# The opening of a long-convolution kernel in one written order, with half-array convolution and turns

## The chip, the cores and the metric

The kernel runs on one core of one Trainium2 chip. The metric is the device time of one execution in microseconds (us); the median of the timed runs counts, and a profiled execution shows where its time goes. The engines are TensorE (PE in the profile, its weight loads PEld), VectorE (DVE), ScalarE (ACT), GpSimd (POOL) and SyncE (SP, which only issues DMAs here).

## The reference

Two layers, each a long convolution block and a dense block, forward and backward. The transforms of the convolution are along time; `kv` and its spectrum depend on no layer's input, so both layers share them.

```python
def _A_ref(q, k, v, shift_k, ssm_k, ssm_D):
    B, S, D = q.shape                      # 1, 2048, 448
    ks = shift_k.shape[-1]                 # 4
    k_pad = jnp.pad(k, ((0, 0), (ks - 1, 0), (0, 0)))
    k_shift = jnp.zeros_like(k)
    for t in range(ks):
        k_shift = k_shift + k_pad[:, t:t + S, :] * shift_k[:, ks - 1 - t][None, None, :]
    kv = k_shift * v
    kv_f = rfft(pad(kv, S), axis=time)     # length 2 S
    kf_f = rfft(pad(ssm_k, S))
    y = irfft(kv_f * kf_f)[:, :S] + kv * ssm_D
    return q * y

def _B_ref(x, w1, w2):
    return silu(x @ w1) @ w2               # D = 448 to F = 1792 and back

x = A_q
x = x + _A_ref(_layernorm(x), A_k, A_v, A_shift_k, A_ssm_k, A_ssm_D)
x = x + _B_ref(_layernorm(x), B_w1, B_w2)
x = x + _A_ref(_layernorm(x), A_k, A_v, A_shift_k, A_ssm_k, A_ssm_D)
x = x + _B_ref(_layernorm(x), B_w1, B_w2)
# outputs: x, and its gradients by grad_out in q, k, v, shift_k, ssm_k, ssm_D, w1, w2
```

## The kernel before

The kernel has three stages. The **opening** (`_ssm_prefix`, L342 on) computes the product of two spectra and turns it back as far as `A1kv`. The **main part** (`Main`) runs the layers forward and backward, with TensorE's order written out by hand. The **suffix** does the gradients of the convolution. The change is in the opening, and in one late load and product that read what the opening stored (L1353 and L1383).

The 4096-point transform is split 128 x 16. A stage of 128 points is a matmul by `M1sb`, a stage of 16 points with real and imaginary parts is a matmul by a 128x128 matrix (`Gsb`, `Gpre`), and between the two the data is turned on TensorE (a "turn" is a set of transposes into PSUM and a copy out of it). All of this passes through PSUM: one tile of four (tag `A`) per step, filled by TensorE and emptied by ACT or DVE. The steps of the opening, with the letters that the written orders use:

- A, a: `ssm_k` (`ksd`, `K_sb`) turned into `Kt` (L398 to L409); D adds `ssm_D` to its first row; B, b: first stage into `A1K` (L411 to L419), which is one half of the array `KAB`.
- G: 16 diagonal matrices 112x112 of the shift's weights (L431). T, t: `k_n` turned into `kT` (L448), 129 positions a row so that a shift by one row of blocks is an offset of one column. C, c: the shifted sum as matmuls of `kT` by the diagonals into `ps_cv` and a copy to `ks` (L467, L470); O: its store `KS_d` (L472); m: its product with `v_n` (L473). S, s: first stage of that into `A1kv` (L483).
- K, k: five groups of `A1K` turned into `Z`, on the halves of the array (L232), and two by DMA (KD, L442). P, p: second stage in place (14 pieces of 1024 columns, L251); Q: for two pieces the store `spec_K` and four DMAs that swap halves into `KAB[:, 0]` (L289).
- Z, z: seven groups of `A1kv` turned into `ZkvA`, `ZkvB` (L542); F, f: second stage in place; U: the stores `spec_KV`, behind two of which the loads of `w1sb` and `w2sb` are issued (L561, L567).
- M: the spectra's products, `pab` (DVE, L572); V, v: the inverse second stage (L260, L261) and the copy to `A1kv`.
- N: the layer norm of the first rows in steps; W: `w2T` by DMA transposes (L452, L453), `Minvsb` (L218) and `gb0` (L516).

In a token of a written order a capital is the work of TensorE or of the issuing engine, a small letter the copy, and its last letter `a` or `d` the engine (ACT, DVE); the numbers name the piece.

Before, the program from the first turn up to about P8 is written as loops, for which the scheduler sets the order of each engine; a load balancer (`_Bal.pick`, L98) gives each copy to ACT or DVE by its estimate of their load. In the loops the channels (d) are split in halves of 224 and in four blocks of 112. Only from there on does `PRODUCTS` fix the order of PE, ACT, DVE and POOL. SP has no written order. `w2T`, `Minvsb` and `gb0` are issued on SP behind the two DMA turns.

Behind the opening, `ys` (L599, `ps_y`) needs all of `A1kv`; then `ps_g` needs `w2T` and `ps_h` needs `w1sb`.

Of the kernel before, what the change touches and what calls it, by code (L numbers as in the profile page):

```python
# [10 lines left out]
FP32 = mybir.dt.float32  # L11
# [6 lines left out]
P = 128  # L18
# [103 lines left out]
PRODUCTS = """  # L122
P9 P10 P11 P12 p9a p10d p11a P13 p12d P8 p8a Z0 Q5 p13d Z1 z0d Z2 z1a Q6 F0 z2d F1 f0a F2 f1d F3 f2a F4 Q4 M0 F5 f3a Z4
f4a Z6 z4d f5a z6d F8 f8a F9 M1 F12 F13 f9a Z5 M2 f12a V0 z5d f13a Z3 v0a F11 z3yd z3xd F7 f11a M3 F6 f7a F10 V1 M4 f6a
V2 f10a M6 V3 v1a M5 V4 v2a M11 V5 v3a V6 M10 v4a V11 M12 v5a V10 M13 v6a V12 v11a M7 V13 v10a M8 V7 v12a M9 V8 v13a v8d
V9 v7a v9a
# [16 lines left out]
def kernel(  # L143
# [33 lines left out]
    k.KS_d = dram.tile([2, P, J, D // 2], BF16, name="KS_d")  # L177
# [87 lines left out]
def _fft_inv_stage2_half(k, pa, pb, B1, ci, psum, cnd):  # L265
    nc = k.nc
    pv = psum.tile([P, 2, 8, 64], FP32, name="ps_v", **k.pt["v"])
    for i in range(8):
        for src, g, first in ((pa, G_IAC, True), (pb, G_IBC, False)):
            for r in range(2):  # L270
                ri = slice(64 * r, 64 * r + 64)
                nc.tensor.matmul(pv[:, r ^ (ci & 1), i, :], lhsT=src[ri, i * P:(i + 1) * P], rhs=k.Gsb[ri, g, ri], start=first, stop=not first)  # L272
    out = (B1[:, :, 32 * ci:32 * ci + 32].rearrange("p q (i h s) -> p h i q s", h=2, s=2) if cnd
           else B1[:, 8 * ci:8 * ci + 8, :].rearrange("p i (q h s) -> p h i q s", h=2, s=2))
    _copy(nc, k.bal.pick(1024), out, pv[:].rearrange("p h i (q s) -> p h i q s", s=2))
# [43 lines left out]
def _ln_steps(k, pool, c, src, si, n_g):  # L319
# [4 lines left out]
    for tl in range(4):  # L324
        k.tc.keep_in_program_order(nc.vector.bn_stats(out=st[:, tl, :], in_=src(tl)))
# [5 lines left out]
        yield  # L331
    for tl in range(4):
        k.tc.keep_in_program_order(nc.vector.tensor_scalar(out=n_g[:, tl, :], in0=src(tl), scalar1=mv[:, tl, 0:1], scalar2=r[:, tl:tl + 1], op0=ALU.subtract, op1=ALU.mult))
        yield
# [6 lines left out]
def _ssm_prefix(k):  # L341
# [4 lines left out]
    with ExitStack() as es:  # L346
# [6 lines left out]
        k.M1sb = k.wk.tile([P, 16, 2, P], BF16, name="M1sb", tag="WX")  # L353
# [15 lines left out]
        skc = spec.tile([DC, ND, 4], FP32, name="skc")  # L369
        skb = spec.tile([DC, ND, 4], BF16, name="skb")  # L370
# [1069 lines left out]
```

## Time and profile before

| | us |
|---|---|
| median of three timed runs | 697.8 (697.25 to 698.92) |
| the profiled execution | 692.97 |
| its span, first to last instruction | 690.9 |
| last copy into `A1kv` ends | 84.7 |
| first `ps_y`, first `ps_g`, first `ps_h` | 84.77, 90.56, 96.47 |

The granted TensorE clock was 0.999 of full speed over the span. A row of the timeline gives start, length, engine, line, operation, what it writes and reads, its shape and how many such instructions follow one another; a length covers them all. Idle time ahead of an instruction stands in square brackets with what ended it. In a table of windows each engine has its busy time and its instructions in brackets; matmuls overlap, so PE's busy time is more than its work. Rows of SPq, ACTq and POOLq are DMAs being issued; the DMA view adds the time from issue to landing.

### The profile page before, as it was taken

The page shows a single profiled execution, that of the slowest core. Times are in us where ns is not written, and L with a number is a line of the kernel's source. Part 1 is how long each engine was busy: PE and PEld are TensorE (multiplying, and loading weights), DVE is VectorE, ACT ScalarE, POOL GpSimd, SP SyncE. Part 2 cuts the span into 40 slices and gives each one's busy share as a digit, 9 for nine tenths or more (in the row PEclk, how much of TensorE's full clock was granted, in tenths as well). Part 3 has the DMA queues.
Part 4 walks back from the last instruction along what each step waited for, and adds up shares of the span by engine and source line. Part 5 has one row for each costly group of instructions (what it writes and reads, how often), then busy time and mean ns, then how long its engine had stood idle before and what let it go on. Part 6 is the DMA issues. An engine that isn't in the chain of part 4 may idle for free.

```text
span 690.9 us, 14461 instructions
## 1 busy us (share of the span) xinstructions
PE 669.0 (97%) x5844; PEld 362.1 (52%) x5879; DVE 481.6 (70%) x1131; ACT 429.9 (62%) x522; POOL 104.8 (15%) x177
## 2 busy tenths in 40 slices
PE   8999999899999999999999999999999999999997
PEld 6876745454434444444444444544555555555666
DVE  5779943667889858899478874843936555538992
ACT  5988976878947868669577585223543543554431
POOL 1057310110011100111001000010111211102311
PEclk9999999999999999999999999999999999999999
DMA  8999978179698777597766789949599988957991
GB/s 320 244 316 321 337 203 220 56 191 259 167 265 233 221 182 176 137 253 219 199 157 183 211 231 354 271 142 210 191 249 342 328 285 315 341 190 223 320 310 42
DMA packets 203956, 162.60 MB, mean 235 GB/s; under 512 B 153505, under 2 KB 184244, under 8 KB 203122
## 3 DMA queue, kind: packets, MB, share of 16 engines
q1 hardware_dynamic: 190806, 113.35, 60.2%
q0 software_dynamic: 11088, 39.84, 16.7%
q10 hardware_dynamic: 1996, 8.49, 3.7%
q8 instruction: 46, 0.75, 0.5%
q14 instruction: 20, 0.16, 0.1%
HBM read 66.05 MB, written 54.60 MB: 175 GB/s over the span
## 4 chain that ended last, share of the span: by engine, by line
PE 64%; DVE 19%; issue 6%; ACT 5%; DMA 3%; POOL 3%; POOLq 0%; ACTq 0%
PE ps_d L1082 25%; PE ps_n L872 8%; PE ps_h L674 6%; PE ps_g L674 6%; PE ps_o L834 5%; DVE ln_st L308 2%; DVE lb_v L1030 2%; PE ps_v L272 2%; POOL rstd L313 2%; DMA spec_K<-KAB 1%; DVE n L316 1%; DVE lb_v L1033 1%; DVE lb_v L1034 1%; DVE X L838 1%; PE ps_h L678 1%
## 5 line engine op out<-in xcount | busy, mean ns | idle before, releaser
L1082 PEld LDWEIGHTS <-dstat 128*128 128x128 bf16 x928 | 87.1, 98 | 75.7 <-issue 4.0
L872 PE MATMUL ps_n<-w1T,ghT 128*128 128x448 bf16 x448 | 96.6, 353 | 2.0 <-DVE ghT L857 1.7
L834 PE MATMUL ps_o<-w2sb,aT 128*128 128x448 bf16 x448 | 89.2, 353 | 0.6 <-DVE X L838 0.6
L674 PE MATMUL ps_h<-nT,w1sb 128*128 128x512 bf16 (+1 forms) x410 | 83.5, 336 | 2.2 <-ACT Dall L116 1.0
L116 ACT CAST ghT<-ps_g 128x1024 bf16<-128x1024 f32 (+1 forms) x54 | 48.4, 900 | 58.3 <-PE ps_g L678 47.7
L674 PE MATMUL ps_g<-nT,w2T 128*128 128x512 bf16 x317 | 77.9, 379 | 2.2 <-DVE Dall L117 0.5
L872 PEld LDWEIGHTS <-ghT 128*128 128x128 bf16 x448 | 41.4, 98 | 50.7 <-DVE ghT L857 6.7
L834 PEld LDWEIGHTS <-aT 128*128 128x128 bf16 x448 | 43.2, 98 | 41.1 <-issue 2.7
L674 PEld LDWEIGHTS <-w1sb 128*128 128x128 bf16 x420 | 39.2, 98 | 36.7 <-issue 7.2
L817 ACT ACTIVATE aT<-ps_h 128x1024 bf16<-128x1024 f32 (+1 forms) x48 | 44.2, 921 | 19.1 <-PE ps_h L674 10.2
L1030 DVE SCALAR_TENSOR_TENSOR lb_v<-lb_u,n 128x448 bf16<-128x448 bf16 x60 | 37.2, 620 | 24.5 <-ACT lb_u L876 24.1
L116 ACT CAST Dall<-ps_h 128x1024 bf16<-128x1024 f32 (+2 forms) x60 | 54.3, 904 | 0.0
L313 POOL TENSOR_TENSOR rstd<-ln_ve,mhalf 128x2 f32<-128x2 f32 (+1 forms) x24 | 19.9, 831 | 225.7 <-DVE ln_ve L312 225.7
L674 PEld LDWEIGHTS <-w2T 128*128 128x128 bf16 x336 | 31.3, 98 | 42.1 <-issue 7.2
L827 ACT ACTIVATE Dall<-Dall 128x1024 bf16<-128x1024 bf16 (+1 forms) x48 | 53.2, 1186 | 0.1
L1082 PE MATMUL ps_d<-X,dstat 128*128 128x448 bf16 x224 | 47.6, 353 | 0.0
L1082 PE MATMUL ps_d<-go,dstat 128*128 128x448 bf16 x224 | 47.2, 353 | 0.0
L1082 PE MATMUL ps_d<-n3m,dstat 128*128 128x448 bf16 (+1 forms) x240 | 47.0, 340 | 0.0
L1082 PE MATMUL ps_d<-n1m,dstat 128*128 128x448 bf16 (+1 forms) x240 | 46.5, 340 | 0.0
L876 ACT ACTIVATE lb_u<-ps_n,rstd 128x448 bf16<-128x448 f32 x32 | 20.5, 640 | 28.9 <-PE ps_n L872 24.3
L116 ACT CAST A1g<-ps_v 128x1024 bf16<-128x1024 f32 x14 | 15.0, 1069 | 36.5 <-PE ps_v L272 36.5
L838 DVE TENSOR_TENSOR X<-X,ps_o 128x448 bf16<-128x448 bf16 x32 | 19.5, 611 | 21.3 <-PE ps_o L834 21.1
(210 smaller groups left out, 1112.4 us busy)
## 6 DMA issues: line engine op xcount, KB each, us to landing
dstat<-a_d SPq DMA_DIRECT2D x28, 512.0 KB, 5.2
dstat<-g_d SPq DMA_DIRECT2D x28, 512.0 KB, 5.8
a_d<-turned SPq DMA_DIRECT2D x16, 512.0 KB, 3.0
g_d<-turned SPq DMA_DIRECT2D x16, 512.0 KB, 3.0
a_d<-turned SPq DMA_DIRECT2D x16, 384.0 KB, 2.7
g_d<-turned SPq DMA_DIRECT2D x16, 384.0 KB, 3.0
spec_K<-KAB POOLq DMA_DIRECT2D x7, 512.0 KB, 5.7
KAB<-KAB POOLq DMA_DIRECT2D x28, 128.0 KB, 5.1
```

The costliest lines, as they stand in the source:

```text
L116: return nc.scalar.copy(out, in_)
L272: nc.tensor.matmul(pv[:, r ^ (ci & 1), i, :], lhsT=src[ri, i * P:(i + 1) * P], rhs=k.Gsb[ri, g, ri], start=first, stop=not first)
L313: nc.gpsimd.tensor_tensor(out=r[:, lo:hi], in0=ve[:, lo:hi], in1=k.mhalf[:, lo:hi], op=ALU.pow)
L674: self.nc.tensor.matmul(ps, lhsT=w[:, b, ft * P:(ft + 1) * P], rhs=x[:, b], start=(start and b == 0), stop=(stop and b == bs[2]))
L817: self.last_silu = nc.scalar.activation(aT[hh][:, o:o + hi - lo, :], ps(lo, hi), ACT.Silu)
L827: self.nc.scalar.activation(dT[hh][:, o:o + n, :], dT[hh][:, o:o + n, :], ACT.Derivative_silu)
L834: nc.tensor.matmul(po[:, :D], lhsT=aT[ft // 7][:, ft % 7, tl * P:(tl + 1) * P], rhs=self.w2sb[:, ft, :], start=(ft == 0), stop=(ft == NF - 1))
L838: self.last_o = nc.vector.tensor_tensor(out=X[:, t, :], in0=X[:, t, :], in1=po[:, :D], op=ALU.add)
L872: nc.tensor.matmul(pn[:, :D], lhsT=gh[ft // 7][:, ft % 7, tl * P:(tl + 1) * P], rhs=self.w1T[:, ft, :], start=(ft == 0), stop=(ft == NF - 1))
L876: nc.scalar.activation(u0[:], pn[:, :D], ACT.Identity, scale=k.rstd[2 * L + 1][:, t:t + 1], accum_out=cp[:, tl, 0:1])
L1030: nc.vector.scalar_tensor_tensor(out=v[:], in0=u0, scalar=-1.0 / D, in1=n_t, op0=ALU.mult, op1=ALU.mult, accum_out=cp[:, 1:2])
L1082: self.nc.tensor.matmul(ps[:, cols], lhsT=st[:, t, :], rhs=mov[:, t, cols], start=(first and t == 0), stop=(last and t == NT - 1))
```

## The change

One order, `OPENING`, replaces the loops and `PRODUCTS`; it covers everything from A0 to the last copy into `A1kv` and fixes PE, ACT, DVE, POOL and SP. Who copies is written into the tokens, and the balancer is out of use there. A token with `h` works on the halves of the array (64 rows of weights at a time, the two halves in turn). With it:

- The channels are split at 256 (CH), and `k_n` is turned in four blocks of 128 (the last overlaps the third); the convolution multiplies 64 rows by 64x64 diagonals: 64 matmuls a piece for h = 0, 48 for h = 1, in place of 32 of 112 rows.
- The diagonals come from two broadcast products (G) on DVE, not from 16 instructions; the `skc` cast on POOL goes, and the shifts come by two loads.
- T3, T0, T2, the K turns, six of seven Z turns, and V4, V11 and V12 are on halves. `kT` is copied out in one piece a turn.
- T stands ahead of part of B; Z0 and Z2 stand ahead of the last piece of S. P, K, C and S are interleaved piece by piece.
- On SP: the two DMA turns, `Minvsb`, `gb0`, the store U0, then w2's two transposes, ahead of which they were before.
- `KS_d` is one array, not two halves; the loads and products that read it follow.

The core of the diff:

```diff
-PRODUCTS = """
...
+OPENING = """
+A0 a0xa G1 A1 a1xd D0 a0ya B01 a1ya B00 b00a B02 A2 b01d G0 a2d B03 b02a b03a A3 a3d B04 b04a B05 b05d B15 B16 B07
+b07d D1 T3h t3d b15a b16a T0h t0a T1 B06 b06a t1d T2h C00 c00a O00 C11 c11a O11 t2d B10 B13 b10a B11 b11a m00 b13d m11
+C03 c03a B17 b17d m03 S110 s110a B12 b12a K0h C12 S001 c12a O12 s001a B14 b14a k0d N0 K2h S030 s030a O03 K1h m12 k2d
+S111 S000 k1d N1 C10 s111a s000a c10a C01 c01a K3h N2 N3 k3d P1 p1a P3 p3a P2 p2d Q1 P4 p4a S031 m01 S120 s031a K4h
+C02 s120a m10 c02a O02 S010 k4d O01 s010d S011 s011a P5 p5d P7 p7a m02 S121 s121a C13 S101 s101a S020 s020a S021 c13d
+O10 m13 P8 p8a s021d S130 s130d P9 KD5 Z0h z0d p9a S100 s100a P0 p0a KD6 W4 W0 Z2h S131 P6 Q2 s131a N4 z2d Q4 Z3h z3xd
+P11 O13 Q0 z3yd P10 N5 p6a Q3 Z4h F0 z4d p11a p10a Z1h Q5 f0a z1d N6 P13 F9 p13a f9a Z5h P12 p12a Q6 F8 F1 z5d f1a U0
+W1 W2 F4 f8d f4d F3 f3a F11 f11a F2 F7 F5 f7a M8 M3 f2a U2 U7 f5a Z6 z6d F6 f6a M0 V3 U6 M4 V8 v3a v8a F10 M9 f10a M6
+F13 F12 f13a f12a V0 V9 V4h M7 M10 V7 U4 v0a V6 M2 v9a V10 v4a V2 M1 U11 M13 M5 M11 U9 v7a v6a v10a v2a V1 v1a V13 V5
+M12 N7 v5d v13a V11h v11a V12h v12a U13
 """
...
-    k.KS_d = dram.tile([2, P, J, D // 2], BF16, name="KS_d")
+    k.KS_d = dram.tile([P, J, D], BF16, name="KS_d")
...
-        k.M1sb = k.wk.tile([P, 16, 2, P], BF16, name="M1sb", tag="WX")
+        m1t = k.wk.tile([P, 16 * 2 * P + ND * 4 * 64], BF16, name="M1sb", tag="WX")
+        k.M1sb = m1t[:, 0:16 * 2 * P].rearrange("p (n c k) -> p n c k", c=2, k=P)
...
-        kT = k.wk.tile([DC, 4, ND, 4, 129], BF16, name="kT", tag="W1")
-        w2o = k.wk.tile([P, 2 * S + ND * 4 * DC], BF16, name="ksd", tag="W2")
+        kT = k.wk.tile([P, 4, ND, 4, 129], BF16, name="kT", tag="W1")
+        w2o = k.wk.tile([P, 2 * S], BF16, name="ksd", tag="W2")
         ksb = [w2o[:, i * S:(i + 1) * S] for i in range(2)]
         ksb += [_hd(k, [P, S], "K_sb")[:] for i in range(2)]
-        diag = w2o[:DC, 2 * S:].rearrange("p (c j d) -> p c j d", c=ND, j=4)
+        diag = m1t[:, 16 * 2 * P:].rearrange("p (c j d) -> p c j d", c=ND, j=4)
...
+        nc.scalar.dma_start(out=skb[:, 0:3, :], in_=k.A_shift_k[0:384, :].rearrange("(c p) j -> p c j", p=P))
+        nc.scalar.dma_start(out=skb[64:128, 3, :], in_=k.A_shift_k[384:448, :])
...
+        CH = ((0, 256), (256, 448))
+        H2 = SPEC // 2
...
+        def A_(part):
+            lo, hi = KPARTS[part]
             n = hi - lo
-            kview = ksb[lo // P][:n].rearrange("p (n1 n2) -> p n2 n1", n2=16)
-            pt = psum.tile([P, 2, 1024], BF16, name="ps_kt", **a_)
-            pv = pt[:, :, 0:8 * n].rearrange("p g (i d) -> p g i d", d=n)
+            kview = ksb[part][:n].rearrange("p (n1 n2) -> p n2 n1", n2=16)
+            pv = bank(("a", part), [P, 2, 1024], "ps_kt", BF16)[:, :, 0:8 * n].rearrange("p g (i d) -> p g i d", d=n)
             for i in range(16):
                 nc.tensor.transpose(pv[:, i // 8, i % 8, :], kview[:, i, :], k.ident[:n, :n])
...
+
+        def a(part, s, e):
+            lo, hi = KPARTS[part]
+            n = hi - lo
+            pv = live["a", part][:, :, 0:8 * n].rearrange("p g (i d) -> p g i d", d=n)
+            gs = {"": slice(0, 2), "x": slice(0, 1), "y": slice(1, 2)}[s]
+            _copy(nc, e, Kt.rearrange("p (g i) d -> p g i d", g=2)[:, gs, :, lo:hi], pv[:, gs])
...
+        def B_(h, i):
+            lo, hi = CH[h]
+            ps = bank(("b", h, i), [P, 2, 2, 256], "ps_s1")
+            for w in range(2):
+                for c in range(2):
+                    nc.tensor.matmul(ps[:, w, c, :hi - lo], lhsT=k.M1sb[:, 2 * i + w, c, :], rhs=Kt[:, 2 * i + w, lo:hi], start=True, stop=True)
...
+        def G_(r):
+            n, rs = 3 + r, slice(64 * r, 64 * r + 64)
+            nc.vector.tensor_tensor(out=diag[rs, 0:n].rearrange("p c j d -> p (c j) d"),
+                                    in0=k.ident[rs, rs].rearrange("p (o d) -> p o d", o=1).broadcast_to((64, 4 * n, 64)),
+                                    in1=skb[rs, 0:n].rearrange("p c (j o) -> p (c j) o", o=1).broadcast_to((64, 4 * n, 64)), op=ALU.mult)
...
+        def turned(key, name, srcs, half):
+            if half:
+                pt = bank(key, [P, 2, 16, 64], name, BF16)
+                for i in range(16):
+                    _turn64(k, pt, i, srcs(i))
+                live[key] = pt[:].rearrange("p r i x -> p i r x")
+            else:
+                pt = bank(key, [P, 16, P], name, BF16)
+                for i in range(16):
+                    nc.tensor.transpose(pt[:, i, :], srcs(i), k.ident[:])
+                live[key] = pt[:].rearrange("p i (r x) -> p i r x", r=2)
...
+        def T_(jq, half):
+            turned(("t", jq), "ps_kT", lambda i: kn[:, 4 * jq + i % 4, GBLK[i // 4][0]:GBLK[i // 4][1]], half)
+
+        def t(jq, s, e):
+            _copy(nc, e, kT[:, jq].rearrange("p c j q -> p (c j) q")[:, :, 1:129].rearrange("p i (r x) -> p r i x", r=2), live["t", jq].rearrange("p i r x -> p r i x"))
...
+        def K_(g, half):
+            turned(("k", g), "ps_tr", lambda i: A1Kf[:, 16 * g + i, :], half)
...
+        def C_(h, jq):
+            pc = bank(("c", h, jq), [P, 4, 4, 64], "ps_cv")
+            at = {(0, 0): 0, (0, 1): 2, (1, 0): 1, (1, 1): 3} if h == 0 else {(2, 0): 1, (2, 1): 2, (3, 1): 3}
             for u in range(4):
                 j = 4 * jq + u
...
+                for e in (2 * h, 2 * h + 1):
+                    for q in range(4):
+                        js = (j - q) % J
+                        src = kT[:, js // 4, e, js % 4, 1:129] if j >= q else kT[:, js // 4, e, js % 4, 0:128]
+                        for r in range(2):
+                            if (e, r) in at:
+                                rs = slice(64 * r, 64 * r + 64)
+                                nc.tensor.matmul(pc[:, at[e, r], u, :], lhsT=src[rs], rhs=diag[rs, e, q, :], start=(q == 0), stop=(q == 3))
...
+        def c_(h, jq, s, e):
+            lo, hi = CH[h]
+            kk = work.tile([P, 2, 4, 256], BF16, name="ks_kv", tag="pab", bufs=4)
+            ks, kvt = kk[:, 0, :, :hi - lo], kk[:, 1, :, :hi - lo]
+            live["m", h, jq] = ks, kvt
+            pc = live["c", h, jq]
+            if h == 0:
+                _copy(nc, e, ks.rearrange("p u (e r d) -> p r e u d", e=2, r=2), pc[:].rearrange("p (r e) u d -> p r e u d", r=2))
+            else:
+                _copy(nc, e, ks.rearrange("p u (x d) -> p x u d", x=3), pc[:, 1:4])
...
+        def O_(h, jq):
+            nc.gpsimd.dma_start(out=k.KS_d[:, 4 * jq:4 * jq + 4, CH[h][0]:CH[h][1]], in_=live["m", h, jq][0])
+
+        def m(h, jq):
+            ks, kvt = live["m", h, jq]
+            nc.vector.tensor_tensor(out=kvt, in0=ks, in1=vn[:, 4 * jq:4 * jq + 4, CH[h][0]:CH[h][1]], op=ALU.mult)
...
+        def U_(lo):
+            hi = min(x for x in (2, 4, 6, 7, 9, 11, 13, 14) if x > lo)
+            (nc.gpsimd if lo else nc.sync).dma_start(out=k.SPEC_d["KV"][:, lo * 1024:hi * 1024], in_=zkv(lo * 1024, hi * 1024))
...
+        def V_(ci, half):
             pab = live["V", ci]
...
+            if half:
+                live["v", ci] = _fft_inv_half(k, pab[:, 1], pab[:, 0], ci, psum)[:].rearrange("p h i (q s) -> p h i q s", s=2)
+            else:
+                live["v", ci] = _fft_inv_stage2_full(k, pab[:, 1], pab[:, 0], ci, psum)[:]
+            live["vh", ci] = half
...
+        def W(i):
+            if i == 0:
+                k.gb0 = _hd(k, [P, 4, D], "gb0")
+                nc.sync.dma_start(out=k.gb0[:], in_=_pm(k.grad_out[0])[:, 0:4, :])
+            elif i == 1:
+                k.w2T = k.wk.tile([P, ND, F], BF16, name="w2T", tag="WY")
+                nc.sync.dma_start_transpose(out=k.w2T[:, 0:3, :], in_=k.B_w2[:, 0:384])
+            elif i == 2:
+                nc.sync.dma_start_transpose(out=k.w2T[:, 3:4, :], in_=k.B_w2[:, 320:448])
+            else:
+                _load_minv(k, nc.sync)
...
+        flat = {"P", "p", "F", "f", "U", "M", "V", "v"}
+        with tc.manual_schedule(engines={e.engine for e in (nc.tensor, nc.scalar, nc.vector, nc.gpsimd, nc.sync)}):
+            for tok in OPENING.split():
+                kind = tok[:next(i for i, x in enumerate(tok) if x.isdigit())]
+                rest = tok[len(kind):]
+                num = "".join(x for x in rest if x.isdigit())
+                args = [int(num)] if kind in flat else [int(x) for x in num]
+                tail = rest[len(num):]
+                if kind in "abtkcszpfv":
+                    args += [tail[:-1], eng[tail[-1]]]
+                elif kind in "TKZV":
+                    args.append(tail == "h")
+                do[kind](*args)
...
-                ksf = sp.tile([P, 2, J, D // 2], BF16, name="ksf")
+                ksf = sp.tile([P, J, D], BF16, name="ksf")
                 with tc.issue_after(k.last_x.ins):
-                    nc.scalar.dma_start(out=ksf[:], in_=k.KS_d[:].rearrange("h p j d -> p h j d"))
+                    nc.scalar.dma_start(out=ksf[:], in_=k.KS_d[:])
```

More of the change, by code (lines that the diff above doesn't have):

```diff
@@ L537, in Q, with Z_ @@
             _swap_halves_dma(k, KAB[:, 0, :], Ka, lo, hi)
-        def Z_(g):
-            pt = live["z", g] = psum.tile([P, 16, P], BF16, name="ps_tr", **a_)
-            for i in range(16):
-                nc.tensor.transpose(pt[:, i, :], B1[:, 16 * g + i, :], k.ident[:])
-        def z(g, part, eng):
-            lo, hi = (8 * part, 8 * part + 8) if g == 3 else (0, 16)
-            _copy(nc, eng, block(g, lo, hi), live["z", g][:, lo:hi, :])
+        def Z_(g, half):
+            turned(("z", g), "ps_tr", lambda i: B1[:, 16 * g + i, :], half)
@@ L590, in _ssm_prefix @@
+        k.xq.append(live["xq"])
         B1v = B1.rearrange("p a (c n s) -> p a c n s", c=2, n=16)
```

233 lines of the change are left out of this document (77 added, 156 removed).

## The prediction

> **What bounds the kernel now.** I read the page's head first, then the opening in windows of 5 us, the engines in order of time there, and the wait view of the first 86 us.
>
> ```profile
> span 690.9 us, 14461 instructions
> ...
> PE 669.0 (97%) x5844; PEld 362.1 (52%) x5879; DVE 481.6 (70%) x1131; ACT 429.9 (62%) x522; POOL 104.8 (15%) x177
> ```
>
> TensorE (PE) carries the whole kernel, so a stage ahead of the main part is worth what it ends earlier. The opening hands over when the last copy into `A1kv` is done, at 84.7 us (ACT, 83.71 + 1.01); the first `ps_y` matmul starts at 84.77. The lists of both programs have the same order on every engine from `ps_y` on, so I count each microsecond of the opening as one of the total. The windows (length, busy time and instructions of PE, PEld, DVE, ACT, POOL, then the granted clock, the DMA share and GB/s):
>
> ```profile
> 30.00:35.00 5.00, 4.83 (x105) 4.64 (x105) 3.64 (x7) 5.00 (x6) 1.10 (x2) 1.00 1.28 191
> 45.00:50.00 5.00, 4.83 (x63) 3.77 (x62) 3.06 (x4) 3.88 (x6) 2.93 (x7) 1.00 1.03 343
> 70.00:75.00 5.00, 4.99 (x75) 4.31 (x75) 5.00 (x6) 5.00 (x7) 3.49 (x7) 1.00 1.00 348
> 75.00:80.00 5.00, 5.00 (x92) 4.93 (x90) 5.00 (x5) 5.00 (x6) 1.65 (x2) 1.00 0.99 317
> 90.00:95.00 5.00, 4.53 (x27) 2.14 (x27) 4.29 (x13) 3.60 (x5) 1.47 (x2) 1.00 0.14 49
> ```
>
> In the last stretch both copy engines, ACT and VectorE (DVE), are full; in the middle they have holes. Four rows of the timeline and two of the wait view (total, times, longest) say how fast they work and what they wait for:
>
> ```profile
> 72.87 10.21 ACT L116 CAST A1kv<-ps_v 128x1024 bf16<-128x1024 f32 x11
> ```
> ```profile
> 74.52 8.03 DVE L572 TENSOR_TENSOR pab<-ZkvB,KAB 128x2048 bf16<-128x2048 bf16 x7
> ```
> ```profile
> 30.55 1.74 PE L467 MATMUL ps_cv<-ksd,kT 112*128 112x112 bf16 x32
> ...
> 33.91 2.46 SPq L453 DMA_TRANSPOSE w2T<-in_B_w_dram  x1
> ```
> ```profile
> DVE ks_kv L473 <- ACT ks_kv L470: 3.7, 4, 1.2
> ACT ks_kv L470 <- PE ps_cv L467: 3.6, 5, 1.0
> ```
>
> Eleven copies in 10.21 us are 0.92 us each (start to start; the last one's full 1.02 taken off), seven products in 8.03 us are 1.14. The convolution's matmuls (1.74 us a piece) hold ACT, and ACT's copy holds DVE. The chain of waits names DMAs for 50.9 to 77.9 us, but DVE's rows have no hole from 69.98 to 83.8 us; I take the copy engines, not the DMAs, as the bound there.
>
> **The copies, summed.** Prices are start to start, from multi-instruction rows of 0 to 85 us. ACT: PSUM fp32 copies of 1024, 896, 768 columns 0.92, 0.84, 0.70; bf16 copies of 2048, 1024, 512 columns 1.77, 0.91, 0.50. DVE: fp32 1.13, 1.00, 0.87; bf16 1.12, 0.64, 0.36; an M product 1.14; a convolution product 0.54 (896), and by its column rate 0.61 (1024) and 0.47 (768).
> - ACT before: 38 x 0.92 + 17 x 0.84 + 4 x 0.70 + 4 x 1.77 + 7 x 0.91 + 0.50 = 66.0. After: 52 x 0.92 + 16 x 0.70 + 1.77 + 3 x 0.91 = 63.5.
> - DVE before: 14 x 1.14 + 12 x 1.13 + 7 x 1.00 + 4 x 0.87 + 7 x 1.12 + 9 x 0.64 + 0.36 + 8 x 0.54, the 16 diagonals 16 x 0.14, and 4.5 for norm and D row = 65.0. After: 14 x 1.14 + 10 x 1.13 + 4 x 0.87 + 15 x 1.12 + 4 x 0.64 + 4 x 0.61 + 4 x 0.47, the two `G` products 1.1, and the same 4.5 = 60.0.
> Three long bf16 turns go from ACT (1.77) to DVE (1.12), 16 small diagonals become two, and K's turns into `kT` are copied in 4 pieces, not 8. `G`'s two broadcast products (64x1024, 64x768) are in no row: 1.1 by the convolution products' rate, 2.0 by the fp32 copies' rate; I take 1.1, since their operands are bf16 in SBUF like the former's. Copies out of half-array turns keep their price: `KAB<-ps_tr` (half turns) takes 1.21 on DVE, `ZkvB<-ps_tr` (full) 1.22.
>
> **TensorE, summed.** Half-array matmuls are in the trace: L232 puts 64 into 1.11 us, 0.017 each against 0.054 for the convolution's, and L272 in the suffix does the same with two accumulating terms. Convolution: 8 x 1.74 = 13.9 becomes 4 x 64 x 0.017 = 4.4 for h = 0, and for h = 1 32 paired (0.55) and 16 that use one half of the array alone. Those alone are bounded by 0.017 and 0.07 (16 K_sb turns, 64*128, 1.2 us); at 0.06 they are 0.96, so 4 x 1.5 = 6.0: 10.4 in all, -3.5. Turns: `T` 3.7 to 2.6, `Z` 6.7 to 4.3, three `V` -1.1. Together -8.1.
>
> Each change between the full array and its halves has a price in the trace:
>
> ```profile
> 24.42 0.41 PE L467 MATMUL ps_cv<-ksd,kT 112*128 112x112 bf16 x5
> 24.77 1.11 PE L232 MATMUL ps_tr<-ident,KAB 64*128 64x64 bf16 x64
> 25.80 0.28 PE L467 MATMUL ps_cv<-ksd,kT 112*128 112x112 bf16 x2
> ```
>
> The fifth L467 starts at 24.64 and L232 0.13 later instead of 0.054; the last L232 starts at 25.69 and L467 0.11 later instead of 0.017: 0.17 us a block of half pieces. The new order has 17 blocks, the old one 3: +2.4. Net -5.7 on PE, which was issuing for some 71 of the 79 us from 5.4 to 84.7. It comes off the end only through shorter waits of the copy engines. The Trainium skill ("TensorEngine Tiling (Array Packing)", Key Properties) speaks against the change here: changing the tiling mode drains TensorE. The gap above agrees; by a rule without a drain PE's sum would be 2.4 lower and the end the same.
>
> **Holes.** From 7.3 us (the first turned block) to 84.7 ACT has 77.4 - 66.0 = 11.4 us of holes: 4.2 up to 24.9, 5.9 up to 57.7, 1.3 behind. After:
> - First stretch. `T` now stands ahead of seven of K's stage-1 pieces. k_n lands at 14.1 and 15.1 us, v_n at 19.9 and 22.1. ACT's nine copies ahead of `t0` are 7.8 us, so it is there at 15.1 and its block is turned about 16.4: 1.3. `c00` then ends at 20.0, behind v_n's first half; `m00`, `b13`, `m11`, S110 give 22.5 and ACT's own row brings it to `s110` at 23.0: no hole. With 0.9 of small waits 2.2 instead of 4.2.
> - Middle. The five waits for the convolution (3.6) shrink with its piece, from 1.74 to 1.1 or 1.5, on average by 0.44 each: 2.2. 5.9 becomes 3.7. Bounds are 5.9 (nothing shrinks) and 1 (as dense as the last stretch); I take the row's.
> - Last stretch: 1.3 again.
> Sum 7.2; the end is 7.3 + 63.5 + 7.2 = 78.0, that is 6.7 us earlier. DVE agrees: from M8 to the handover it has 14 products, z6, one norm step and v5, 18.6 us and a tail of 2, so M8 must start at 57.4; 41.4 us of work stand ahead of it from 7.3, which leaves 8.7 of holes, where before its first product (60.97) there were 10.3.
>
> **What is moved.** On SP Minvsb and gb0 go ahead of w2's transposes, which now stand behind U0's store, so behind f0 and f1. Behind f1 ACT has 22 copies, 20.2 us: f1 ends near 57. They issue for 6.83 + 2.46 = 9.3 us, so end near 67; nothing else is queued there before w1T, which waited to 94.48 for another reason. The first `ps_g` needs w2T 5.9 us behind the handover, at 84. What hides them is 17 us of products and copies. Without that cover they cost a microsecond for each they are late. On POOL Q1, Q2, Q4 go first, with KS_d stores between; a Q holds POOL for 3.3 us on average (2.5 to 4.6), seven are 23 us in a stretch of some 30: no bound. w1sb is asked for 15 us ahead of the handover (11.2 before; 12 to land, first needed 11.8 behind it). The removed `skc` cast and the new second load of the shifts (ACT, behind its table load, 3 us + at most 5.1 as Drow) end before DVE is wanted at 8.3. KS_d in one layout changes one late load and one product's access: nothing.
>
> **Rivals.**
> 1. The holes stay: in-order queues hand every wait on, and 11.4 us remain. 7.3 + 63.5 + 11.4 = 82.2: -2.5. For it: four PSUM tiles serve all streams as before. Against: PE is relieved by 5.7 us. The same page of the Trainium skill (PSUM Bottleneck) states this case as a rule: tiling speeds TensorE but not the evacuation of PSUM; the full windows of ACT and DVE from 70 us agree, the holes before them don't.
> 2. Dense: 4 us of holes, as if the last stretch's rate held nearly throughout: 74.8, -9.9. For it: the windows from 70 us show that the engines can. Against: k_n and v_n land no earlier, and the DMAs, at share 1.0 from 5 to 90 us, move the same bytes.
> 3. w2's transposes meet Q6's swaps. Where w2T is turned in the old order the DMAs move 191 GB/s (30 to 35 us), against 348 at 70 to 75. Q6 follows p12, one copy ahead of f1, so both start near 57. M13 (DVE, 7 us before the handover) needs Q6 at 71.0; its swaps take 2.5 to issue and 5.1 to land, 64.6. If they take as long as the slowest load of the opening (w2sb, 16.2), they land at 75.7 and DVE stands 4.7: 82.7, -2.0. Against: KS_d's stores beside the old transposes landed in 5.3.
> 4. Slower: the convolution's half pieces don't reach L272's rate. Its weights start at column 0 or 1 of rows of 129, L232's and L272's at multiples of 128. At 0.054 a matmul the old convolution shows no price for that; at 0.017 no row does. At 0.054 the 448 half pieces cost 24.3 us instead of 10.4, PE's sum is 71 - 5.7 + 13.9 = 79.2, and PE is the bound: 5.4 + 79.2 and 2 (dense) to 8.3 (as before) of holes, 86.6 to 92.9; with 4, 88.6, +3.9. It decides from about 0.046 a matmul on, where PE's sum of 76 and 4 of holes reach 86. Against: the old convolution and the full turns (both 0.054 to 0.058) differ in alignment and not in price.
>
> **How the numbers follow.** The profiled execution took 692.97 (span 690.9 and 2.1 around it); the forecast makes it 686.3. The median of the three timed runs is 697.8, 4.8 above; I carry the difference: 697.8 - 6.7 = 691.1. Chances: forecast (-8.5 to -4.5) 0.44; rival 1, 0.16, 695.3; rival 2, 0.18, 687.9; rival 3, 0.06, 695.8; rival 4, 0.09, 701.7; mixtures that come to nothing 0.07, 697.8. Faster by over 0.2% (1.4 us, about what a measurement of this kernel can tell from no change) 0.84, within it 0.07, slower 0.09. The range leaves out rival 4 and the far half of rival 2: 687.3 to 698.0.
>
> **What would show it.** Last copy into `A1kv` near 78 us; ACT with 63 to 64 us of copies before it and about 7 of holes, DVE 60; a convolution piece of 1.1 and 1.5 us; M8 near 57; W1 near 57, w2T down by 70 and no wait of `ps_g` for it. It is wrong if ACT's holes between 24 and 50 us are over 5, if DVE stands before a product for a swap, if the convolution runs at 0.05 a matmul, or if the handover is earlier and the main part gives it back.

## The result, and the profile after

The changed kernel is slower: 737.6 us, the median of six runs (721.5 to 748.4), against 697.4 for six runs of the kernel before on the same chip. The ratio, 1.0356 with a 95% interval of 1.0311 to 1.0401, goes by the two shortest runs (721.5 and 722.1), since the others, the profiled one among them, show a lower clock, so the lengths read below tell where the loss lies and not its exact size. The forecast was 691.1. In the profiled execution (742.0, span 740.0) the opening's last copy into `A1kv` ends at 115.3 us instead of 84.7, and what follows takes 624.7 instead of 606.2.

The page's head and then the windows of the same stretches as before:

```profile
span 740.0 us, 15235 instructions
...
PE 671.8 (91%) x6263; PEld 357.5 (48%) x6263; DVE 478.4 (65%) x1110; ACT 427.7 (58%) x523; POOL 105.5 (14%) x175
```
```profile
30.00:35.00 5.00, 4.98 (x215) 4.34 (x205) 4.81 (x9) 5.00 (x7) 1.49 (x2) 1.00 0.70 162
45.00:50.00 5.00, 4.81 (x81) 3.13 (x81) 4.97 (x7) 4.87 (x6) 4.33 (x7) 1.00 0.98 301
70.00:75.00 5.00, 2.74 (x68) 2.34 (x65) 0.92 (x1) 5.00 (x7) 0.49 (x1) 1.00 1.04 96
75.00:80.00 5.00, 0.00 (x0) 0.00 (x0) 0.00 (x0) 0.51 (x1) 0.52 (x2) 0.68 1.38 113
90.00:95.00 5.00, 0.00 (x0) 0.00 (x0) 0.00 (x0) 0.00 (x0) 0.23 (x1) 0.54 1.18 202
```

At 45 us the copy engines are as full as forecast. From 70 us on first VectorE and TensorE and then ScalarE stand for long stretches, while the DMAs are busy (share over 1) and move 96 to 202 GB/s where there were 317 and 348 from 70 to 80 us before. The granted clock (seventh figure) falls to about 0.5 in the idle stretches, and TensorE restarts slowly: from 83.8 us its matmuls into `ps_v` start 0.107 us apart, from 87.0 on 0.055. The timeline says which transfers these are, and what waits:

```profile
61.28 30.71 SPq L610 DMA_TRANSPOSE w2T<-in_B_w_dram  x1
...
79.36 0.49 POOL L300 DMA_DIRECT2D KAB<-KAB  x1 [6.43 <-DMA KAB<-KAB]
```
```profile
82.47 1.22 DVE L578 TENSOR_TENSOR pab<-ZkvB,KAB 128x2048 bf16<-128x2048 bf16 x1 [11.56 <-DMA KAB<-KAB]
...
107.50 1.23 DVE L578 TENSOR_TENSOR pab<-ZkvB,KAB 128x2048 bf16<-128x2048 bf16 x1 [21.53 <-DMA w1sb<-in_B_w_dram]
```
```profile
92.04 27.67 SPq L612 DMA_TRANSPOSE w2T<-in_B_w_dram  x1
```

w2's two transposes took 6.83 + 2.46 us to issue before; now they take 30.71 + 27.67. The wait of 21.53 is put down to a load of `w1sb`, which this product does not read: it reads `ZkvB` and `KAB`, so it waits for the last swap, and a store of POOL's that waited 10.39 for `DMA KAB<-KAB` starts at 107.57. ACT's last copies:

```profile
113.39 1.93 ACT L116 CAST A1kv<-ps_v 128x1024 bf16<-128x1024 f32 x2 [1.67 <-PE ps_v L278]
```

The DMA view of 60 to 112 us (KB each, median us from issue to landing) has both sides of it; the swaps took 5.1 before, and POOL's stores and loads, not shown here, take 19 to 29:

```profile
KAB<-KAB POOLq DMA_DIRECT2D x11, 128.0 KB, 16.3
...
w2T<-in_B_w_dram SPq DMA_TRANSPOSE x2, 48.0
```

Behind the opening X stood 14.7 us for the late stores `spec_KV` (0.7 before) and `ps_g` 6.7 for `w2T`.

### The profile page after: what moved, and what is told of

Its sections match the earlier page's. It is cut to its first block, busy times and chain, and to the rows that moved or that the text cites. A ratio compares the mean times of both kernels' runs of the same rounds, so it can differ in the third digit from the quotient of the medians.

```text
span 740.0 us, 15235 instructions
## 1 busy us (share of the span) xinstructions
PE 671.8 (91%) x6263; PEld 357.5 (48%) x6263; DVE 478.4 (65%) x1110; ACT 427.7 (58%) x523; POOL 105.5 (14%) x175
## 4 chain that ended last, share of the span: by engine, by line
PE 59%; DVE 16%; DMA 14%; issue 5%; ACT 3%; POOL 2%; SPq 0%; POOLq 0%; DVEq 0%; ACTq 0%
PE ps_d L1125 23%; PE ps_n L915 7%; PE ps_h L717 6%; PE ps_g L717 5%; PE ps_o L877 5%; DMA spec_KV<-ZkvA 4%; DMA spec_KV<-ZkvB 3%; DMA KAB<-KAB 3%; DVE ln_st L319 2%; DVE lb_v L1073 2%; PE ps_v L278 2%; POOL rstd L324 2%; DMA k_n<-in_A_k_dram 2%; DMA spec_K<-KAB 2%; DVE n L327 1%
## 5 line engine op out<-in xcount | busy, mean ns | idle before, releaser
L1125 PEld LDWEIGHTS <-dstat 128*128 128x128 bf16 x928 | 87.1, 98 | 75.7 <-issue 4.0
L717 PE MATMUL ps_g<-nT,w2T 128*128 128x512 bf16 x336 | 81.0, 384 | 7.4 <-DMA w2T<-in_B_w_dram 6.7
L266 PE MATMUL ps_v<-Gpre,pab 128*128 128x128 bf16 x88 | 13.6, 252 | 32.3 <-DVE pab L578 31.5
```

The source lines that it names most:

```text
L717: self.nc.tensor.matmul(ps, lhsT=w[:, b, ft * P:(ft + 1) * P], rhs=x[:, b], start=(start and b == 0), stop=(stop and b == bs[2]))
L1125: self.nc.tensor.matmul(ps[:, cols], lhsT=st[:, t, :], rhs=mov[:, t, cols], start=(first and t == 0), stop=(last and t == NT - 1))
```

## The experiments

Theory A: w2's transposes and POOL's swaps, in flight together, hold each other up. Rivals at first: a new order that is worse by itself, too many bytes at one time, the stores in place of the swaps. Each experiment names the kernel it starts from; of the lines of `OPENING` the diffs show only the tokens around the change.

**1. w2's transposes early** (from the changed kernel)
```diff
-O11 t2d B10 B13
+O11 t2d W1 W2 B10 B13
...
-z5d f1a U0 W1 W2 F4
+z5d f1a U0 F4
```


> The changed kernel with w2's two DMA transposes back ahead of the two DMA turns, behind K's turns into kT (they issue near 21 us); nothing else differs. Theory A, the transposes and POOL's DMAs stop each other: w2T takes 9 to 11 us again, no product waits for a swap, the last copy into A1kv ends at 78 to 83 us, the time is 688 to 696 us, faster than before. Rival B, the written order and the half pieces are slow themselves (the holes at 15 to 17 and 35 to 38 us show it): the opening ends at 87 us or later and the time stays above 700.

707.8 us, ratio 1.0171 (1.0138 to 1.0203): about half of the loss goes, no product waits for a swap any more, and the opening ends at 89.3, not at 115.3. The time is still the one that rival B named (87 or later, above 700), not theory A's. Two new things show. In the middle of the convolution TensorE stands, with its operands there (timeline of TensorE):

```profile
34.84 1.19 PE L506 MATMUL ps_cv<-M1sb,kT 64*128 64x64 bf16 x27 [5.71 <-issue]
```

"issue" means that nothing the profile shows was waited for. And the main part is later by itself, 616.5 us behind the opening in place of 606.2:

```profile
93.86 1.71 ACT L643 CAST Ysb<-ps_y 128x896 bf16<-128x896 f32 x2 [4.57 <-DMA spec_KV<-ZkvA]
...
101.48 0.62 DVE L764 TENSOR_TENSOR X<-x0c,a_t 128x896 bf16<-128x896 bf16 x1 [6.05 <-DMA spec_KV<-ZkvB]
```

Ysb and X lie where `ZkvA` and `ZkvB` were, and the written order puts some of the stores that free these behind the loads of `w1sb` and `w2sb` on POOL.

**2. The old kernel with w2's transposes late**, on SP behind the first `spec_KV` store, which goes to SP for it; Minvsb is issued earlier by that.
```diff
-        nc.sync.dma_start_transpose(out=k.w2T[:, 0:3, :], in_=k.B_w2[:, 0:384])
...
+                    if lo == 0:
+                        nc.sync.dma_start_transpose(out=k.w2T[:, 0:3, :], in_=k.B_w2[:, 0:384])
+                        nc.sync.dma_start_transpose(out=k.w2T[:, 3:4, :], in_=k.B_w2[:, 320:448])
```


> The kernel before with w2's transposes behind the first spec_KV store, which goes to SP as in the change (Minvsb's load, no longer held back by them, moves ahead of the two DMA turns). Theory A: w2T takes 30 to 60 us, the swaps 15 us and more, and the time is 720 to 745 us with the old order and the old matmuls. Rival B: within 3 us of 697.

736.2 us, ratio 1.0586 (1.0536 to 1.0636). That move costs the old kernel 41 us, and its rows look like the changed kernel's:

```profile
64.56 29.04 SPq L555 DMA_TRANSPOSE w2T<-in_B_w_dram  x1
93.66 19.24 SPq L556 DMA_TRANSPOSE w2T<-in_B_w_dram  x1
```

**3. The same bytes, not transposed** (from the changed kernel; the second transpose is replaced likewise)
```diff
-nc.sync.dma_start_transpose(out=k.w2T[:, 0:3, :], in_=k.B_w2[:, 0:384])
+nc.sync.dma_start(out=k.w2T[:, 0:3, :], in_=k.B_w1[0:384, :].rearrange("(c p) f -> p c f", p=P))
```


> The changed kernel, but w2T is filled at the same place by plain loads of the same bytes (rows of w1 in place of w2 turned, so what is computed with w2T is another product). Theory A, it is the transposing: the loads land in 10 to 20 us, no product waits for a swap for over 3 us, and the time is 688 to 697 us. Rival C, it is 1.8 MB more in a stretch where the DMAs are full: still 715 or more.

707.5 us, ratio 1.0174 (1.0124 to 1.0223): half of the loss goes with the transposing, at the same bytes. The time lies above theory A's 697 and below the bytes' 715. The bytes are not free there either: products waited 8.0 us for swaps.

**4. Stores on SP, behind the transposes**: all `spec_KV` stores and the loads of `w1sb`, `w2sb` go to SP (from the changed kernel), so that of POOL's transfers the transposes meet only the last swaps and the stores `spec_K` issued among them.
```diff
-            (nc.gpsimd if lo else nc.sync).dma_start(out=k.SPEC_d["KV"][:, lo * 1024:hi * 1024], in_=zkv(lo * 1024, hi * 1024))
+            nc.sync.dma_start(out=k.SPEC_d["KV"][:, lo * 1024:hi * 1024], in_=zkv(lo * 1024, hi * 1024))
```


> The changed kernel with all spec_KV stores and the loads of w1sb and w2sb on SP behind w2's transposes, so that the transposes meet only the last swaps of POOL. Theory A: once POOL's last swaps are through, the transposes run at their old rate: w2T is done 15 to 30 us after its issue instead of 57, the opening ends at 80 to 95 us and the time is 700 to 720 us, part of it waits for w1sb. Rival C (bytes): the transposes are as slow as in the change only if the stores run beside them, so w2T in 10 us and the opening at 78 to 80.

723.8 us, ratio 1.0409 (1.0353 to 1.0465), more than the 700 to 720 expected. This company suffices, without the later `spec_KV` stores and the loads: the first transpose meets it and takes 29 us. The second is issued at 93.4, some 4 us ahead of the last swap's landing, and takes 4.65.

```profile
63.97 29.37 SPq L610 DMA_TRANSPOSE w2T<-in_B_w_dram  x1
93.39 4.65 SPq L612 DMA_TRANSPOSE w2T<-in_B_w_dram  x1
```

**5. The loads last** (from 1): W5 and W6 are the loads of `w1sb` and `w2sb`, no longer behind U6 and U9.
```diff
-V7 U4 v0a
+V7 U4 W5 v0a
...
-v12a U13
+v12a U13 W6
```


> The run with w2's transposes early (707.8 us) plus one move: the load of w1 goes behind the fourth group of spec_KV stores and the load of w2 behind the last one, on POOL. In that run Ysb stood 4.6 us and X 6.1 us for spec_KV stores that POOL had queued behind these loads. Theory 'queue order': both waits go, X waits under 1.5 us, and the time falls by 5 to 10 us, to 698 to 703. Rival 'bandwidth': the stores are late because the bytes of both transfers share the DMA engines, whatever the order; then some 2 us go and the time stays at 705 to 708. Rival 'needed earlier': the products with w1 and w2 then wait for their loads, and what the stores give back is lost there.

701.7 us, ratio 1.0073 (1.0036 to 1.0109). Ysb's wait is gone; X still waits 4.9.

**6. No DMA transposes in the opening** (from 5): w2T as in 3, and
```diff
-P9 KD5 Z0h z0d p9a S100
+P9 K5h Z0h z0d p9a k5d S100
...
-KD6 W4 W0 Z2h S131
+K6h W4 W0 Z2h k6a S131
```


> The same, and no DMA transpose is left in the opening: w2T is filled by plain loads of w1's rows (another product is computed), and K's turns 5 and 6 are done by TensorE in halves, copied by VectorE and ScalarE (about 1.2 us each). In the run with early transposes TensorE stood 5.7 + 1.5 + 2.3 us for nothing that the profile shows, each time until a DMA transpose ended. Theory 'transposes starve TensorE of instructions': these standstills go (under 1 us left in all), the opening's last copy comes some 6 us earlier than with the transposes, and the time falls 4 to 7 us against the run beside it with the loads last. Rival 'too many instructions': TensorE stands because the halves need twice as many instructions as it is given, whatever the DMA does; then 5 us or more of standing remain and the time is the same or longer by the added copies (1 to 2 us).

696.7 us, ratio 1.0020 (0.9992 to 1.0049). TensorE's standstills "issue" fall from 8.3 to 2.6 us; 2.2 of them are left beside plain loads.

**7. Full turns** (from 5): the letter `h` dropped on every T, K and Z, as in
```diff
-D1 T3h t3d b15a b16a T0h
+D1 T3 t3d b15a b16a T0
```


> The run with the loads last, with all turns of k, K and the product on the whole array again (16 instructions for a block in place of 32); the convolution keeps its halves, and the DMA transposes stay. TensorE needs some 200 instructions fewer in the first 50 us. Theory 'transposes starve TensorE of instructions': the standstills come at about the same transposes but are shorter, since what was fetched lasts longer: 4 to 8 us in place of 9.5, and the time is within 3 us of the run with the loads last either way. Rival 'halves are worth what the forecast says' (0.7 to 0.8 us a block for the whole array against the halves, 17 blocks): TensorE gets longer by 3 to 6 us and the time too.

702.8 us, ratio 1.0104 (1.0072 to 1.0137), not to be told from 5's. The standstills fall to 4.4 us. In sum the halves of the turns bring no time that can be measured: full turns keep TensorE longer, but they spare 3.9 us of standstills.

**8. The transposes behind the last swap** (from the changed kernel)
```diff
 k.w2T = k.wk.tile([P, ND, F], BF16, name="w2T", tag="WY")
+nc.sync.dma_start(out=k.w2T[:, 0, 0:64], in_=KAB[:, 0, 14 * 1024 - 64:14 * 1024])
```


> The changed kernel with one added transfer: ahead of w2's transposes SP copies the last 64 columns of K's swapped spectrum into w2T (the transposes then overwrite them), so that the transposes start only when the last of POOL's swaps has landed, about 77 to 80 us. Theory 'any software-queue transfer': the transposes then meet POOL's spec_KV stores and loads instead and take 20 us or more each, the stores as long: 720 us or more. Rival 'only the swaps': the two transposes take 8 to 12 us together beside the stores, w2T is there by 92 us, the stores land in under 12 us, and the time is 700 to 708.

704.8 us, ratio 1.0119 (1.0082 to 1.0155). Behind the swaps the two transposes take 11.03 + 1.57 us, far less than 58. That does not clear POOL's stores and loads, though. The first transpose starts at 84.6, when the last `spec_KV` stores and the load of `w2sb` are in flight until about 93. The DMA view of 84.6 to 92.6 us, and then of 92.6 to 100.6 (q0 has POOL's transfers, q1 the transposes; packets, MB, time of the packets as a share of the 16 engines):

```profile
q0 software_dynamic: 579, 2.26, 76.9%
q1 hardware_dynamic: 701, 0.18, 32.0%
```
```profile
q1 hardware_dynamic: 6531, 1.66, 98.4%
```

Beside them the transposes moved 0.18 MB in 8 us, and 1.66 MB in the 8 us behind them. Experiment 2 has the same company for longer. Its last swap lands at 102.9 us, and from 104 to 116 POOL has only `spec_KV` stores and the load of `w1sb` in flight:

```profile
q1 hardware_dynamic: 1623, 0.41, 119.5%
q0 software_dynamic: 80, 0.34, 6.8%
```

Here both sides crawl, at some 30 GB/s each, with no swap in flight. So the swaps are not needed for the collision: stores and loads of POOL's do it too. Why POOL's side crawls in the one case and not in the other is open.

With the transposes behind the swaps the opening ends at 81.4, which shows what the new order is worth: 3.3 us. The main part then gives it back: TensorE stands 8.6 us ahead of `ps_g`, and X and Ysb wait 6.4 and 4.0 for stores.

**9. The old kernel with more instructions**
```diff
-        k.nc.tensor.transpose(pt[:, r, i, :], src[rs], k.ident[rs, rs])
+        for _ in range(2):
+            k.nc.tensor.transpose(pt[:, r, i, :], src[rs], k.ident[rs, rs])
```


> The kernel before, with every turn in halves issued twice over the same words of PSUM (the opening's turns of K: 160 more turns and as many more weight loads in the first 60 us, some 0.55 us of TensorE for each block). Its 16 us of DMA transposes (20 to 36 us) stand where they stood, and nothing else is changed. Theory 'TensorE runs out of instructions while DMA transposes run': TensorE now shows standstills for no reason in the profile, 1.5 us or more in one piece, between 20 and 38 us, where the old kernel has none of that length. Rival 'the standstills come from the new order, not from how many instructions there are': none over 0.8 us, and the time grows by no more than the doubled turns, 2 to 3 us.

705.0 us, ratio 1.0138 (1.0092 to 1.0185). The old order, which had no such standstill, now has three, beside its DMA transposes (issued from 21 to 37 us) or right behind them:

```profile
28.49 0.35 PE L233 MATMUL ps_tr<-ident,KAB 64*128 64x64 bf16 x11 [1.35 <-issue]
...
33.32 0.82 PE L233 MATMUL ps_tr<-ident,KAB 64*128 64x64 bf16 x43 [1.44 <-issue]
...
39.79 0.69 PE L233 MATMUL ps_tr<-ident,KAB 64*128 64x64 bf16 x19 [2.43 <-issue]
```

Cut the windows at these restarts and count (length, then busy time and instructions of PE and of PEld, then DVE, ACT, POOL, clock, DMA):

```profile
28.45:33.30 4.85, 3.39 (x128) 3.15 (x128) 1.62 (x4) 2.67 (x2) 0.56 (x1) 1.00 1.18 204
33.30:39.75 6.45, 4.04 (x128) 3.80 (x128) 3.27 (x5) 3.49 (x3) 0.54 (x1) 1.00 1.28 223
```

Each stretch has 128 matmuls and 128 weight loads, 256 instructions. In experiment 13, another order, the stretches between restarts have the same count, or twice it:

```profile
25.40:29.90 4.50, 3.22 (x128) 2.90 (x128) 3.69 (x6) 2.69 (x4) 0.63 (x1) 1.00 1.18 231
29.90:37.50 7.60, 7.05 (x256) 5.88 (x256) 6.25 (x13) 6.71 (x8) 1.86 (x3) 1.00 0.82 173
```

In experiment 1 they have 128 + 128 and 256 + 256. The section on DMA queues of the profile's page has a queue of kind "instruction" (packets, MB), before and after:

```profile
q8 instruction: 46, 0.75, 0.5%
```
```profile
q8 instruction: 49, 0.80, 0.5%
```

TensorE's matmuls and weight loads, divided by 256, are 45.8 and 48.9, so one packet, of some 16 KB, goes with each 256 of them. In experiment 1 such a packet moves at 32.2 to 32.4 us, in the midst of the standstill from 29.1 to 34.8. So TensorE stops when a block of 256 instructions is used up and the next has not come. The Trainium skill ("Runtime: NRT & Kernel Launch", Instruction fetch mechanics) states such blocks, of 16 KiB and fetched by DMA, and calls their cost mostly hidden. The counts and the packets agree; hidden it was not, at 9.4 us in experiment 1.

**10. T later, stores first** (from 5)
```diff
-b07d D1 T3h t3d b15a b16a T0h t0a T1 B06 b06a t1d T2h
+b07d D1 B06 b15a B10 b16a T3h b06a T0h t3d b10a T1 t0a t1d T2h
```
and W5 goes from U4 to ahead of W6, behind all stores.


> The run with the loads last (701.7 us), with two blocks of K's first stage moved ahead of k's turns on TensorE, so that TensorE has 1.1 us of work while it waits for k (there 2.3 us, every engine standing), and with both loads of w1 and w2 behind all spec_KV stores (there X waited 4.9 us for the last stores, which shared the queue with w1's load). Theory: the wait for k_n falls to about 1.2 us, X's wait to 2 us or less, and the time to 696.5 to 699.5. Rival: the end of the opening hangs on the standstills beside the DMA transposes and on POOL's swaps alone, an earlier k is waited out there, and only X's part (2 to 3 us) shows, 698 to 700; or the loads of w1 and w2 are then late for the dense layers, and the time stays above 700.

696.0 us, ratio 0.9989 (0.9961 to 1.0016): level with the kernel before. X no longer waits, and from the opening's end the rest takes 606.1 us again (611.3 in 5). The wait for `k_n` falls from 2.3 to 1.0, but the opening ends at 87.9 as in 5 (87.7): as the rival said of it, T's new place brings nothing that the profiles show. The gain is that of the stores.

**11. w2's transposes in four pieces** (from 10), three of them behind a small read of K's turned blocks:
```diff
+nc.sync.dma_start(out=k.w2T[:, 0:4:3, lo:lo + 32], in_=Z[:, 16 * (0, 2, 1)[i - 8]:16 * (0, 2, 1)[i - 8] + 2, 0:32])
+nc.sync.dma_start_transpose(out=k.w2T[:, 0:3, lo:hi], in_=k.B_w2[lo:hi, 0:384])
+nc.sync.dma_start_transpose(out=k.w2T[:, 3:4, lo:hi], in_=k.B_w2[lo:hi, 320:448])
```


> The run before this one, with w2's transposes cut into four pieces of 448 rows (about 2.4 us each); the second, third and fourth wait behind a small transfer that reads K's block 0, 2 or 1 after its copy, so that there are gaps of some us between them. Theory 'TensorE runs out of instructions while DMA transposes run': what it has fetched lasts 2 to 4 us, so a piece is bridged: the standstill of 5.7 us in the convolution falls under 2 us in all (the one beside K's own transposes, 2.2 us, stays), and the time falls by 2 to 5 us. Rival 'the transposed bytes decide': the same standstill in sum, 4 us or more, spread over the pieces, and no gain; or the last pieces meet the first swaps and both get long, as in the changed kernel.

710.5 us, ratio 1.0224 (1.0181 to 1.0267). The convolution's standstill falls from 5.7 to 1.1, but a copy waits 6.9 for such a read, and K's own DMA turns, now later, meet the first swaps and the stores among them:

```profile
46.77 16.70 SPq L492 DMA_TRANSPOSE KAB<-KAB  x2
```

(6.1 us in experiment 10.) The collision of theory A, with other transposes and at another place.

**12. K's turns 5 and 6 on TensorE** (from 10): the edit of KD5 and KD6 in 6 alone; w2's transposes stay.


> The run with k's turns later, and K's turns 5 and 6 by TensorE in halves (0.64 us each, copies of 1.2 us on VectorE and ScalarE) in place of the DMA's. w2's transposes stay whole. Theory: the standstill of 2.2 us beside K's transposes goes and the copies put 1.2 us on each engine's sum: the time is the same to 1.5 us shorter. Rival: the copies cost more than the standstill, since the copies' engines set the opening's end: 1 to 2 us longer.

697.2 us, ratio 1.0024 (1.0000 to 1.0047): no gain, and no DMA transpose of the opening is left that could meet the swaps.

**13 and 14. Two and three pieces** (from 12), the later ones behind a read of a few bytes of `A1kv`, as in this part of 13:
```diff
+nc.sync.dma_start(out=k.w2T[:, 0:4:3, lo:lo + 2], in_=A1kv[:, 128, 0, 4:4 + 2, :])
+nc.sync.dma_start_transpose(out=k.w2T[:, 0:3, lo:hi], in_=k.B_w2[lo:hi, 0:384])
```


> The run with K's turns 5 and 6 on TensorE (697.2 us), with w2's transposes cut in two pieces of 896 rows (some 5 us each); the second waits behind a transfer of a few bytes that reads the first-stage product copied at about 27 us (nothing writes over what it reads before the inverse transforms' copies). In the run with four pieces the gaps took the convolution's standstill from 5.7 to 1.1 us, but K's own transposes then met POOL's swaps (16.7 us), and a copy waited 6.9 us for a gate's read; both are gone here. Theory 'what was fetched lasts some us': the standstill of 5.4 us falls to 2 to 4 us, and the time by 1.5 to 3.5 us, to 693.5 to 695.5, under the kernel before. Rival 'the second piece starts later and stands in TensorE's way later': the sum of standstills stays at 5 us or more, and the time within 1 us of 697.

692.4 us, ratio 0.9940 (0.9915 to 0.9965): faster than both kernels, by 3.9 us against the one before. The standstill in the convolution fell to 1.3 us, but one of 4.1 came at 37 us, so their sum (5.9) hardly fell: here the time agrees with the theory and the sum with the rival. By the profiles the opening ends at 86.0, 1.8 earlier than in 12, so not all of the gain on 12 is accounted for. Against the kernel before the profiles show no gain at all: there the opening ends at 84.7 and the rest takes 606.2 us, here 606.0. The gain is that of the medians of 9 and 19 runs; where it lies is open.


> The same with three pieces (640, 640 and 512 rows, 3.5 us and less), the third behind a product copied some 5 us later. Theory: standstills under 2 us in all, time 692.5 to 694.5, some 3 us of the forecast's gain back. Rival: the third piece ends at 40 us or later and meets the first of POOL's swaps, it and they then take over 10 us, and the time is 700 or more.

694.6 us, ratio 0.9974 (0.9951 to 0.9998), standstills 2.6: fewer, and no shorter time. POOL waited 5.0 for a store, products 2.9 for swaps; the third piece stands close ahead of the first swaps.

## Why the prediction was wrong

**The step that failed** is "They issue for 6.83 + 2.46 = 9.3 us, so end near 67", and the sentence that 17 us of products and copies hide it. The duration came from a row where the transposes met `KS_d` stores, and was carried to a place where they meet POOL's swaps, and behind these its stores and loads. There it is 58 us (48 in the old kernel, experiment 2), and the swaps that products wait for are late with it. **Rival 3** named the mechanism with 0.06 and mis-sized it: I let the swaps take as long as the slowest load (16.2), which gave 75.7 for the last landing and a gain still; the product behind it started at 107.5. What I set against it, that `KS_d`'s stores landed in 5.3 beside the old transposes, is true, but POOL moved only 0.44 MB there (27.0 to 36.4 us, beside 1.74 MB of transposes); experiments 8 and 2 show that stores, too, can hold transposes up. The 191 GB/s beside the old transposes was the warning; I priced it only on the swaps and kept the transposes at their old length.

**The order on POOL**, "no bound": it bound in two ways. The swaps ran to 79 us (they themselves were held up), and w1sb "asked for 15 us ahead" came ahead of stores that Ysb and X wait for. Moving the loads behind the stores gave some 7 us (0.98 points, experiments 1 and 5); in experiment 10, with the load of `w1sb` behind all stores, X's last wait went too.

**The opening's end, 78.0.** Without the collision it is 81.4 (experiment 8), so 3.3 us of the 6.7 were there. Up to 70 us the changed kernel runs as forecast, but about 4 us late: M8 starts at 61.35 (forecast 57.4), W1 at 61.28 (57). Two holes of together 5.2 us account for it. For the first I had 1.3 us of ACT's time, the second was no term of mine:

```profile
17.27 1.11 PE L238 MATMUL ps_kT<-ident,k_n 64*128 64x64 bf16 x64 [2.35 <-DMA k_n<-in_A_k_dram]
...
38.11 0.82 PE L257 MATMUL ps_s<-KAB,Gpre 128*128 128x512 bf16 x3 [2.86 <-issue]
```

In the first TensorE waited for `k_n`, which I had put at 15.1 us, now that T stands ahead of part of B; the second is the instruction supply beside K's DMA turns.

**The terms that held.** The convolution's half pieces run at the rate I took, and rival 4 is false (its sum 5.4 + 76 + 4 is 85.4, not 86, and nothing hangs on it):

```profile
42.52 1.14 PE L506 MATMUL ps_cv<-M1sb,kT 64*128 64x64 bf16 x64
...
45.94 1.11 PE L506 MATMUL ps_cv<-M1sb,kT 64*128 64x64 bf16 x48
```

A piece of h = 1 (48) takes 1.11, under the 1.5 I took. The waits for the convolution shrank as said, more in fact (wait view to 85 us; 3.6 and 3.7 before):

```profile
ACT ks_kv L116 <- PE ps_cv L506: 1.6, 2, 1.1
DVE ks_kv L524 <- ACT ks_kv L116: 1.0, 1, 1.0
```

The two `G` products took 1.22 + 0.93 = 2.15 us: the upper bound, not the 1.1 I chose. The copies' sum cannot be read apart from the stalls in the changed kernel; in experiment 13, with the copy of one more turn, ACT is busy 67.5 us from 6.4 to 86.0 and stands 12.1, against holes of 7.2 in the forecast, nearly all of them ahead of 57 us. **Rival 1** (the holes stay, 82.2) is thus nearer to the order's own worth (81.4) than the forecast, but by its number alone: the holes that could be named are `k_n` and the instruction supply, not the handing on of waits that it gave as the reason. "TensorE's sum comes off the end only through shorter waits" held, and experiment 7 shows the size for the turns: nothing to be measured, in sum with the standstills.

**The main part unchanged**: its instruction order was, but not its waits. X's 14.7 and `ps_g`'s 6.7 us are waits on what the opening left unfinished, and counting each microsecond of the opening as one of the total missed them.

By the ratios the loss divides as follows: w2's transposes beside POOL's transfers 1.8 points of 3.6 (net of the standstills that they bring at the earlier place), the order on POOL's queue 1.8 (1.0 and 0.8, experiments 5 and 10); pieces and K's turns on TensorE then gave 0.5 more.

## What to carry to other kernels

A DMA's duration belongs to its neighbours: before moving one, list every transfer that is in flight at the new place, by kind, and take its time from a row with the same company. A DMA transpose is kept away from a stretch in which POOL's queue has much in flight, copies within SBUF, stores or loads. Many small instructions on TensorE beside DMA transposes can run its instruction supply dry, so look for waits on "issue" and count the instructions between two restarts.

## What the runs showed of the hardware

- DMA transposes issued from SP and DMAs issued from POOL hold each other up: 9.3 us became 48 to 58, swaps 5.1 became 16.3, and the DMAs, busy, moved 96 to 202 GB/s in the windows shown. It is not the swaps alone: beside POOL's stores and a load the transposes moved 0.18 MB in 8 us (experiment 8) and 0.41 MB in 12 us (experiment 2), and alone 1.66 MB in 8 us. Beside 0.44 MB of `KS_d` stores in the kernel before it was not so, and with plain loads in the transposes' place (experiment 3) the kernel lost 1.7% and not 3.6%. Why is not shown. The Trainium skill ("DMA: Bandwidth & Descriptors", Rules for kernel authors) has "A transpose next to ordinary DMAs needs nothing"; that may hold for the order of the data, but for the time these runs show the opposite.
- TensorE's instructions come in blocks of 256 (46 and 49 packets for 45.8 and 48.9 blocks), and beside DMA transposes a block came up to 5.7 us late. In 13 one came 4.1 us late with the transposes already issued; their packets still ran to 39 us there. Without DMA transposes, beside plain loads, the longest was 2.2 us (experiment 6).
